# Order of the border loads, the V conversion and the kv products in an attention and MLP kernel

## The chip, the cores and the metric

The kernel runs on one core of one Trainium2 chip. The metric is device time in microseconds (us) of that core, as the median of a few runs. Engines are named as in the profile: PE (TensorE products), PEld (its weight loads), DVE (VectorE), ACT (ScalarE), POOL (GpSimd), SP (SyncE, which issues every transfer of this kernel).

## What is computed

```python
# attention without softmax, 8 batches, 8 heads, 576 rows, 64 columns
kv  = einsum('bhsd,bhse->bhde', k, v)
x   = einsum('bhsd,bhde->bhse', q, kv);  x = x / rms(x) * g_norm
# first block: low-rank mixing over the sequence, then channels 512 -> 2048 -> 512
u   = x + (x.T @ U @ V).T               # U is 576 x 32, V is 32 x 576
x   = u + maximum(u @ w_ch1, 0) @ w_ch2
# second block: gated MLP with a 576 x 576 product over the sequence
h   = gelu(x @ w_in);  uu, v = halves of h
out = x + (uu * (w_sg @ layernorm(v) + b_sg)) @ w_out
```

All is float32. U, V and the weights arrive as 64-bit floats, and the kernel turns them into float32 itself (`convert`). The large products are split into a high and a low part of each operand and done as three products (`three`: high by high, high by low, low by high).

## The kernel before

**Stages.** (1) Per batch b: kv products (`att_kv`), five chunks c of x (`att_x`), root and norm (`att_root`, `att_norm`), the low-rank mixing (`att_t` by U, `att_u` by V), and the first 6 of 16 slices of `w_ch1` (`ch1`, two units "U" a slice, one for each half of the sequence). Batch b+1's attention runs between the units of batch b, by the list `PERIOD`, and for b = 0 by the shorter list `FIRST`, since batch 1's x products are already done ahead of it. (2) The other ten slices as a seven-product scheme on blocks of 1024 tokens (`Unit`). Its results go to DRAM (`yd`). (3) `w_ch2`: nine blocks of 512 tokens with eight steps each (`ch2`, two slices f a step); the weights were converted in stage 2, kept in DRAM (`wd`) and are brought back by `load_w2`. (4) The gated MLP.

**What sets the order.** PE runs in the order in which the program stands. On the other engines and in SP's queue a planner orders at build time: among the instructions that its own timing holds ready it takes the one that stands first in the program. Each engine then runs its list strictly in that order. `behind` (`keep_in_program_order`) pins an instruction behind the instruction that stands just before it in the program on the same engine; `convert` and the stores of weight slices are pinned so. `converted` first writes out the conversion of a slice and only then, by `flush`, the store of the slice before it: the store's ACT copy and its subtraction (on POOL for odd slices f, on DVE for even ones) stand behind the next slice's conversion.

**The front, lines 470 to 525.** kv, U and V, and q of batch 0 are loaded; U is converted and stored; then both halves of V, each converted and stored (lines 485 to 488), then kv products of batch 0, `att_x(0, c)`, `att_root(0)`, kv products of batch 1, norms. The loop over `cs` does chunks 0 and 1, 2 and 3, then 4: `att_t(0, c)`, `att_x(1, c)` and, twice, `split_w` of slices 0 and 1. Then `att_u(0, d)` for four d (line 336 multiplies by V, line 344 makes the low part `ul`), `att_root(1)`, `split_w(2)`, the norms of batch 1's first chunks, `split_w(3)`. Slices 4 and 5 are split after the first and third unit of batch 0, and the last store comes after the fifth. The tile `sq` of `att_x` (line 275) has one buffer. PSUM has four buffers "ar", which the kv, x and u products share. In `FIRST`, "K2" is the kv product of batch 2's pair 2; each of K0 and K1 also issues the load of the pair after next (line 553).

**The border of stages 2 and 3, lines 693 to 807.** The last three units are interleaved, and their results leave through SP's queue. w2 slices 8 to 11 are loaded after the pair of units before them, 12 to 15 at product b7 of the last three, 0 to 7 at the border, since their tiles lie on memory of stage 2. `load_y(j, i)` brings two slices of y for a step and splits them into `yx` (ACT line 752, DVE line 753). The first block begins with i = 4, whose y and i = 5's are already on the chip (tile `y0`), so step 2 (i = 6) is the first that needs a y transfer in stage 3. `load_z1(1)` uses `y0`'s buffer.

```python
    load_y(*steps[0])
    load_z1(0)
    load_y(*steps[1])
    for f in range(8):
        load_w2(f)
    for at_, (j, i) in enumerate(steps):
        if 2 <= at_ + 1 < len(steps):
            load_y(*steps[at_ + 1])
```

Of the kernel before, what the change touches and what calls it, by code (L numbers as in the profile page):

```python
# [12 lines left out]
F32 = mybir.dt.float32  # L13
# [9 lines left out]
B, H, S, D = 8, 8, 576, 64  # L23
DM, DFF, RANK = 512, 2048, 32
# [35 lines left out]
def tile_kernel(ctx: ExitStack, tc: tile.TileContext, kvm, kvr, qt, gcol, uv, w12,  # L60
# [21 lines left out]
    def in_turn(*chains):  # L82

        end = object()
        while chains:
            chains = [steps for steps in chains if next(steps, end) is not end]
# [9 lines left out]
    def convert(raw, tmp):  # L96

        low, high = raw[:, :, 0], raw[:, :, 1]
        t = tmp.bitcast(I32)
        behind(nc.scalar.activation(tmp, high.bitcast(F32), AF.Abs))
        behind(nc.scalar.activation(low, low.bitcast(U32), AF.Copy, scale=2.0 ** -29))
        yield
        yield behind(nc.vector.tensor_scalar(tmp, tmp, 2.0 ** -15, 122879.9921875, ALU.max, ALU.min))
        yield behind(nc.vector.tensor_scalar(t, t, 3, 0x3FFFFFF8, ALU.logical_shift_left, ALU.bitwise_and))
        yield behind(nc.vector.scalar_tensor_tensor(t, high, -0x40000000, t, ALU.bitwise_and, ALU.bitwise_or))  # L108
        yield behind(nc.gpsimd.tensor_add(t, t, low))  # L109
# [9 lines left out]
    def flush():  # L119
        while queue:  # L120
            queue.pop(0)()
# [28 lines left out]
    def slot(i, shape, dt, name):  # L150

        return px["wa" if i < 14 else "xa"].tile([P] + shape, dt, tag=f"s{i}", name=f"{name}{i}")
# [49 lines left out]
    def split_w(f):  # L202
        w = slot(f, [2, DM], F32R, "w")
        wh[f], wl[f] = w[:, 0], w[:, 1]
        sub = nc.gpsimd if f % 2 else nc.vector
        converted(w_raw.pop((f, 0)), next_tmp(), split_to(w[:, 0], w[:, 1], sub))
# [39 lines left out]
    def att_kv(b, ps):  # L246
        if ps[0] == 0:
            at_s["kv", b] = pm.tile([P, NP, D], F32, tag="ar", bufs=4, name="kvps")
        acc = at_s["kv", b]
        for p in ps:  # L250
            m, r = kv_t.pop((b, p))
            for c in range(NC):
                src = m[:, c] if c < 4 else r
                for j in range(2):
                    mm(acc[j * D:(j + 1) * D, p, :], src[:, j * D:(j + 1) * D],
                       src[:, P + j * D:P + (j + 1) * D], start=(c == 0), stop=(c == NC - 1))
# [7 lines left out]
    def att_x(b, c):  # L264

        n = rows(c)
        if c == 0:
            at_s["ss", b] = small(b, "ss", 0)
            nc.gpsimd.memset(at_s["ss", b][64:, 4], 1.0)
        ps = pm.tile([P, H, D], F32, tag="ar", bufs=4, name="xps")  # L270
        for p in range(NP):
            mm(ps[:n, 2 * p:2 * p + 2, :], q_t[b, p][:, c * P:c * P + n], kvbd[:, p, :],  # L272
               start=True, stop=True)
        xn = xn_of(b, c)
        sq = ap.tile([P, H, D], F32, tag="sq", name="sq")
        nc.scalar.activation(sq[:n], ps[:n], AF.Square)
        nc.scalar.activation(xn[:n], ps[:n], AF.Copy)
        nc.vector.tensor_reduce(at_s["ss", b][:n, c], sq[:n], AX.X, ALU.add)
        at_s["x", b, c] = xn

    def att_root(b):
        ss = at_s.pop(("ss", b))
        y, t = (small(b, n, i) for i, n in ((1, "ny"), (2, "nt")))
        a, y2, t2 = (i.rearrange("p w h -> p (w h)") for i in (ss, y, t))
        nc.vector.tensor_scalar(a, a, 1.0 / D, EPS, ALU.mult, ALU.add)
        in_turn(rsqrt(y2, t2, a))
        at_s["y", b] = y

    def att_norm(b, cs):

        y = at_s["y", b]
        for c in cs:
            n = rows(c)
            xn = at_s["x", b, c]
            nc.vector.tensor_tensor(xn[:n], xn[:n], y[:n, c].unsqueeze(2).to_broadcast([n, H, D]),
                                    ALU.mult)
            xf = xn.rearrange("p h d -> p (h d)")
            xh = ap.tile([P, DM], F32R, tag="xh", bufs=2, name="xh")
            xl = xh[n:] if c == 4 else ap.tile([P, DM], F32R, tag="xl", bufs=2, name="xl")
            nc.scalar.activation(xh[:n], xf[:n], AF.Copy)  # L300
            nc.vector.tensor_sub(xl[:n], xf[:n], xh[:n].bitcast(F32))
            at_s["x", b, c] = xf, xh, xl
# [72 lines left out]
    def store_v(c, x):  # L375
        nc.scalar.activation(v4[:, c], x, AF.Copy)
        nc.gpsimd.tensor_sub(v4[64:96, c], x[64:96], v4[64:96, c].bitcast(F32))
# [104 lines left out]
    tmp_u = next_tmp()[:, :nu]  # L482
    in_turn(convert(uvr[0][:, :nu], tmp_u))
    store_u(tmp_u)
    tmp_v = [slot(i, [2, DM], F32, "tmpv")[:, 0, :HS] for i in (6, 7)]
    for h, (r, t) in enumerate(zip((uvr[0][:, nu:], uvr[1]), tmp_v)):
        in_turn(convert(r, t))
        store_v(slice(h * HS, (h + 1) * HS), t)
    att_kv(0, list(range(NP)))
    put_kv(0)  # L490
    for p in range(NP):
# [6 lines left out]
    for f in range(1, NA):  # L498
        load_w(f, 0)
    att_root(0)  # L500
    att_kv(1, list(range(NP)))
    put_kv(1)
    att_norm(0, (0, 1))
    for cs in ((0, 1), (2, 3), (4,)):
        if cs[0]:
            att_norm(0, cs)
        for c in cs:
            att_t(0, c)
        for c in cs:
            att_x(1, c)  # L510
        if cs[0] < 4:
            split_w(cs[0] // 2)
    for p in range(2):
        load_kv(2, p)
    for d in range(ND):
        att_u(0, d)
    att_root(1)
    for p in range(NP):
        load_q(2, p)
    split_w(2)  # L520
    att_norm(1, (0, 1))
    split_w(3)

    PERIOD = "X0 X1 X2 X3 U X4 U U K0 U K1 U T0 T1 U U T2 T3 U U T4 U K2 U K3 U D0 D1 D2 D3".split()
    FIRST = "U U U K0 U K1 U T0 T1 U U T2 T3 U U T4 U K2 U K3 U D0 D1 D2 D3".split()
    for b in range(B):
        n, n2 = (i if i < B else None for i in (b + 1, b + 2))
        i = 0
# [161 lines left out]
    while units:  # L690
        n = 3 if len(units) == 3 else 2
        two, units = units[:n], units[n:]
        a, b = two[0], two[-1]
        if n == 3:
            for s in "a5 a1 b5 b1 a3 a6 b3 b6 c5 c1 a7 b7 a2 c3 c6 b2 a4 c7 b4 c2 c4".split():
                two["abc".index(s[0])].product(int(s[1]))
                if s == "b7":
                    for f in range(12, 16):
                        load_w2(f)
        else:  # L700
            for x, p in ((a, 5), (a, 1), (b, 5), (b, 1), (a, 3), (a, 6), (b, 3), (b, 6), (a, 7), (b, 7),
                         (a, 2), (b, 2), (a, 4), (b, 4)):
                x.product(p)
        if b.j == len(BLOCKS) - 1 and b.i in (0, 1):
            y = up.tile([P, ND, S], F32, tag="u32", bufs=2, name="y0")
            y_at.append(y.rearrange("p d s -> p (d s)")[:, :2 * 2 * BT].rearrange("p (a f t) -> p a f t", a=2, f=2))
            for k in range(2):
                nc.sync.dma_start(y_at[0][:, k], yd[0][:, 8 + 2 * k:10 + 2 * k])
        if b.j == len(BLOCKS) - 1 and b.i == 1:
            for f in range(8, 12):  # L710
                load_w2(f)
    flush()
    pha.close()
# [25 lines left out]
    def load_z1(b):  # L739
        zt[b] = up.tile([P, ND, S], F32, tag="u32", bufs=2, name="z32")  # L740
        nc.sync.dma_start(zt[b], ud[b])
# [31 lines left out]
    steps = [(j, (i + 4) % 8) for j in range(NB) for i in range(8)]  # L773
    load_y(*steps[0])
    px["wb"] = wb = ph1.enter_context(tc.tile_pool(name="wb", bufs=1, side="left", reuse_waits="tile"))
    load_z1(0)
    load_y(*steps[1])
    for f in range(8):
        load_w2(f)
    for at_, (j, i) in enumerate(steps):  # L780
        if 2 <= at_ + 1 < len(steps):
            load_y(*steps[at_ + 1])
        step = at_ % 8
        if step == 0 and j + 1 < B:
            load_z1(j + 1)
        for k in range(2):
            ch2(j, 2 * i + k, step == 0 and k == 0, step == 7 and k == 1)
        if j == 0 and step == 5:
            raws = prepare_sg()
        if j == 1 and step < 5:  # L790
            split_sg(step, raws[step])
        if j == NB - 2 and step in (0, 1, 2, 3, 4, 5):
            if step == 0:
                load_wio(0)
            load_wio(step + 1)
            split_wio(step)
        if j == NB - 1:
            if 1 <= step < 7:
                if step < 6:
                    load_wio(step + 6)  # L800
                split_wio(step + 5)
            elif step == 7:
                flush()
            if step >= 3 and step < 7:
                split_z(0, step - 3, zt[order[0]][:, step - 3], nc.vector)
        if step == 7:
            z_out(j)
# [277 lines left out]
```

## Time and profile before

| | |
|---|---|
| median of 3 runs | 1395.4 us (1394.03 to 1396.19) |
| the profiled execution | 1394.67 us |
| its span, first to last instruction | 1392.7 us |
| PE busy | 1346.4 us, 97% of the span |
| DVE, ACT, POOL busy | 771.3, 536.5, 284.2 us |

Times within the kernel are microseconds from the start of the span. The profile holds one execution. A busy PE is one with a product in flight, whatever its clock: the granted clock (1.00 is 2.4 GHz, 0.50 is 1.2 GHz) has a column of its own.

### The profile page before, as it was taken

How to read it: one execution, taken by the hardware profiler on the slowest of the kernel's cores; microseconds unless marked ns; L12 is line 12 of the kernel's file. 1: busy time of each engine (PE TensorE's matmuls, PEld its weight loads, DVE VectorE, ACT ScalarE, POOL GpSimd, SP SyncE). 2: the span in 40 equal slices, each digit the busy share in tenths (PEclk: the TensorE clock that was granted, in tenths of full speed). 3: DMA queues.
4: the chain of work that ended last, by engine and by line, in shares of the span. 5: the costliest groups of instructions: out<-in, count | busy, mean ns of one | idle time of the engine just before them, and what ended most of it. 6: DMA issues, size and time to landing. Idle time of an engine off the chain costs nothing.

```text
span 1392.7 us, 20749 instructions
## 1 busy us (share of the span) xinstructions
PE 1346.4 (97%) x8050; PEld 1177.5 (85%) x8050; DVE 771.3 (55%) x1405; ACT 536.5 (39%) x888; POOL 284.2 (20%) x268
## 2 busy tenths in 40 slices
PE   5799999999999999899999999999999999999998
PEld 4689999997777788688888888888999999999998
DVE  3757777755766732222322223456676775775874
ACT  3656656654554532212112122454333333423321
POOL 1211111100111100200000000336253453543332
PEclk9899999999999999999999999999999999999999
DMA  9556665355766777635434554631020120110001
GB/s 325 189 165 215 220 215 179 132 174 194 252 228 223 243 268 276 238 96 170 146 118 159 163 169 145 210 122 44 1 68 19 51 69 18 52 44 26 35 17 52
DMA packets 86930, 199.44 MB, mean 143 GB/s; under 512 B 12208, under 2 KB 33456, under 8 KB 85040
## 3 DMA queue, kind: packets, MB, share of 16 engines
q1 hardware_dynamic: 86832, 198.12, 42.9%
q8 instruction: 63, 1.03, 0.3%
q14 instruction: 35, 0.29, 0.1%
HBM read 126.00 MB, written 72.09 MB: 142 GB/s over the span
## 4 chain that ended last, share of the span: by engine, by line
PE 83%; DVE 5%; DMA 3%; ACT 2%; issue 1%; POOL 1%; SPq 0%; DVEq 0%; ACTq 0%; POOLq 0%
PE acc L348 9%; PE acc L347 9%; PE acc L349 9%; PE uso L936 8%; PE uso L957 6%; PE uso L848 5%; PE c L347 3%; PE c L348 3%; PE c L349 3%; PE y L347 3%; PE y L348 3%; PE y L349 3%; PE v L347 2%; PE v L348 2%; PE v L349 2%; PE xps L272 2%
## 5 line engine op out<-in xcount | busy, mean ns | idle before, releaser
L347 PE MATMUL acc<-yx,w 128*128 128x512 f32 x576 | 225.3, 391 | 5.9 <-ACT yx L752 5.9
L348 PE MATMUL acc<-yx,w 128*128 128x512 f32 x576 | 225.7, 392 | 1.5 <-DVE yx L753 1.5
L753 DVE SCALAR_TENSOR_TENSOR yx<-yr,yx 128x1024 fp32r<-128x1024 f32 x70 | 86.1, 1230 | 254.2 <-ACT yx L752 249.8
L349 PE MATMUL acc<-yx,w 128*128 128x512 f32 x576 | 225.3, 391 | 0.0
L752 ACT ACTIVATE yx<-yr 128x1024 fp32r<-128x1024 f32 x70 | 74.3, 1061 | 286.9 <-PE acc L349 267.0
L347 PEld LDWEIGHTS acc<-yx,w 128*128 128x128 f32 x576 | 108.8, 189 | 29.3 <-ACT yx L752 6.6
L348 PEld LDWEIGHTS acc<-yx,w 128*128 128x128 f32 x576 | 108.8, 189 | 24.7 <-DVE yx L753 2.1
L349 PEld LDWEIGHTS acc<-yx,w 128*128 128x128 f32 x576 | 108.9, 189 | 22.7
L349 PE MATMUL c<-uh,w 128*128 128x288 f32 x384 | 114.0, 297 | 6.6 <-POOL w L126 6.6
L347 PE MATMUL c<-uh,w 128*128 128x288 f32 x384 | 117.2, 305 | 0.0
L348 PE MATMUL c<-ul,w 128*128 128x288 f32 x384 | 114.1, 297 | 1.8 <-DVE ul L344 1.8
L848 PE MATMUL uso<-zh,wio 128*128 128x288 f32 x512 | 94.1, 298 | 0.8 <-DVE g2u L856 0.7
L957 PE MATMUL uso<-gh,wio 128*128 128x288 f32 x512 | 93.1, 296 | 0.0
L109 POOL TENSOR_TENSOR tmp<-tmp,wior 128x512 int32<-128x512 int32 x12 | 15.7, 1307 | 332.2 <-DVE tmp L108 287.2
L957 PEld LDWEIGHTS uso<-gh,wio 128*128 128x128 f32 x512 | 77.9, 188 | 2.3 <-issue 0.2
L347 PE MATMUL y<-T,c 128*128 128x512 f32 (+1 forms) x200 | 75.3, 377 | 4.0 <-DVE y L595 3.7
L848 PEld LDWEIGHTS uso<-zh,wio 128*128 128x128 f32 x512 | 76.3, 188 | 3.4 <-PE uso L936 1.4
L349 PEld LDWEIGHTS c<-uh,w 128*128 128x128 f32 x384 | 72.6, 189 | 7.1 <-POOL w L126 7.1
L348 PEld LDWEIGHTS c<-ul,w 128*128 128x128 f32 x384 | 72.6, 189 | 3.9 <-DVE ul L344 3.0
L347 PEld LDWEIGHTS c<-uh,w 128*128 128x128 f32 x384 | 72.5, 189 | 3.2 <-issue 1.0
L349 PE MATMUL y<-T,c 128*128 128x512 f32 (+1 forms) x200 | 74.5, 372 | 0.0
L348 PE MATMUL y<-T,c 128*128 128x512 f32 (+1 forms) x200 | 74.4, 372 | 0.0
(206 smaller groups left out, 2912.4 us busy)
## 6 DMA issues: line engine op xcount, KB each, us to landing
yr<-yd SPq DMA_DIRECT2D x70, 512.0 KB, 3.6
yd<-y SPq DMA_DIRECT2D x92, 256.0 KB, 3.5
kvm<-kvm_dram SPq DMA_DIRECT2D x28, 512.0 KB, 4.6
raw<-w_dram SPq DMA_DIRECT2D x26, 512.0 KB, 4.2
q<-qt_dram SPq DMA_DIRECT2D x32, 288.0 KB, 4.6
ud<-ut SPq DMA_DIRECT2D x32, 288.0 KB, 2.2
z<-ud SPq DMA_DIRECT2D x8, 1152.0 KB, 6.9
out_dram<-ot SPq DMA_DIRECT2D x31, 288.0 KB, 2.1
```

The costliest lines, as they stand in the source:

```text
L109: yield behind(nc.gpsimd.tensor_add(t, t, low))
L272: mm(ps[:n, 2 * p:2 * p + 2, :], q_t[b, p][:, c * P:c * P + n], kvbd[:, p, :], start=True, stop=True)
L347: mm(ps, ah, bh, start=start, stop=False, **kw)
L348: mm(ps, ah, bl, start=False, stop=False, **kw)
L349: mm(ps, al, bh, start=False, stop=stop, **kw)
L752: nc.scalar.activation(yh, y, AF.Relu)
L753: nc.vector.scalar_tensor_tensor(yl, y, 0.0, yh.bitcast(F32), ALU.max, ALU.subtract)
L848: mm(ps[:, e, :HS], a[:, s], c[:, halves[e]], start=(d == 0 and i == 0), stop=(d == ND - 1 and i == 2))
L936: mm(ps[:, e, :HS], a[:, s], w[:, halves[e]], start=(c == 0 and i == 0), stop=(c == NC - 1 and i == 1))
L957: mm(ops[d][:, e, :HS], a[:, s], c[:, f, halves[e]], start=(f == 0 and i == 0), stop=(f == ND - 1 and i == 2))
```

## The change

```diff
@@ att_x
-        sq = ap.tile([P, H, D], F32, tag="sq", name="sq")
+        if b or c % 2 == 0:
+            sq = ap.tile([P, H, D], F32, tag="sq", name="sq")
+        else:
+            sq = spare[4][:, 2700:2700 + DM].rearrange("p (h d) -> p h d", h=H)
@@ the front
     store_u(tmp_u)
-    tmp_v = [slot(i, [2, DM], F32, "tmpv")[:, 0, :HS] for i in (6, 7)]
-    for h, (r, t) in enumerate(zip((uvr[0][:, nu:], uvr[1]), tmp_v)):
-        in_turn(convert(r, t))
-        store_v(slice(h * HS, (h + 1) * HS), t)
     att_kv(0, list(range(NP)))
...
     att_root(0)
+    tmp_v = [slot(i, [2, DM], F32, "tmpv")[:, 0, :HS] for i in (6, 7)]
+    uv_in = [convert(r, t) for r, t in zip((uvr[0][:, nu:], uvr[1]), tmp_v)]
     att_kv(1, list(range(NP)))
...
         if cs[0]:
             att_norm(0, cs)
+        if cs[0] == 2:
+            in_turn(*uv_in)
...
             split_w(cs[0] // 2)
+        if cs[0] == 4:
+            for h, t in enumerate(tmp_v):
+                store_v(slice(h * HS, (h + 1) * HS), t)
+            flush()
...
         att_u(0, d)
+    split_w(2)
+    split_w(3)
     att_root(1)
...
-    split_w(2)
     att_norm(1, (0, 1))
-    split_w(3)
...
-    FIRST = "U U U K0 U K1 U T0 T1 U U T2 T3 U U T4 U K2 U K3 U D0 D1 D2 D3".split()
+    FIRST = "U U K0 U K1 U U U T0 T1 U K2 U K3 T2 T3 U U T4 U U D0 D1 D2 D3".split()
@@ stage 2, after product b7 of the last three units
-                    for f in range(12, 16):
+                    for f in range(11, 14):
@@ stage 2, after the pair of units before them
-            for f in range(8, 12):
+            for f in range(8, 11):
@@ the border
     load_y(*steps[0])
-    load_z1(0)
     load_y(*steps[1])
-    for f in range(8):
-        load_w2(f)
+    later_loads = [lambda f=f: load_w2(f) for f in (14, 15)] + [lambda: load_z1(0)] + [lambda f=f: load_w2(f) for f in range(8)]
+    later_loads.pop(0)()
+    later_loads.pop(0)()
     for at_, (j, i) in enumerate(steps):
         if 2 <= at_ + 1 < len(steps):
             load_y(*steps[at_ + 1])
+        for _ in range(3):
+            if later_loads:
+                later_loads.pop(0)()
```

V is converted behind the norms of chunks 2 and 3 and stored behind chunk 4; the store of slice 1 follows there; slices 2 and 3 are split ahead of `att_root(1)`; the squares of batch 0's odd chunks get a second place; the kv products of batch 2 stand further apart. At the border the loads that the first steps don't need stand three to a step between the y loads.

## Rows read from the trace of the kernel before

**Rows 1.** The page, its first part: busy time, share, instructions.

```profile
PE 1346.4 (97%) x8050; PEld 1177.5 (85%) x8050; DVE 771.3 (55%) x1405; ACT 536.5 (39%) x888; POOL 284.2 (20%) x268
```

**Rows 2.** PE's waits: line, waited for, us in total, times, longest.

```profile
PE c L349 <- POOL w L126: 6.6, 2, 6.2
```

**Rows 3.** ACT in order of time: start, us, what, [idle before <- releaser].

```profile
19.10 0.44 ACT L376 ACTIVATE v<-tmpv 128x288 fp32r<-128x288 f32 x1 [1.80 <-POOL tmpv L109]
20.16 0.58 ACT L276 ACTIVATE sq<-xps 128x512 f32<-128x512 f32 x1
```

**Rows 4.** DVE in order of time.

```profile
27.66 0.68 DVE L278 TENSOR_REDUCE spare<-sq 64x8 f32<-64x512 f32 x1 [0.72 <-ACT sq L276]
40.76 0.43 DVE L106 TENSOR_SCALAR tmp<-tmp 128x512 f32<-128x512 f32 x1
41.69 0.69 DVE L108 SCALAR_TENSOR_TENSOR tmp<-spare,tmp 128x512 int32<-128x512 int32 x1
51.95 0.76 DVE L344 TENSOR_TENSOR ul<-ut,uh 128x576 fp32r<-128x576 f32 x1
```

**Rows 5.** PE in order of time, up to the first product by V.

```profile
14.53 7.86 PE L272 MATMUL xps<-kvbd,q 128*128 128x128 f32 x40 [1.22 <-DMA q<-qt_dram]
33.11 0.79 PE L310 MATMUL tp<-xh,u 128*128 128x512 f32 x1 [5.58 <-ACT xh L300]
43.85 0.36 PE L336 MATMUL ups<-v,t 128*128 128x256 f32 x1 [1.21 <-DVE t L316]
```

**Rows 6.** Instructions on V's temporary by stretch: DVE, ACT, POOL busy (count), clock.

```profile
16.00:24.00 8.00, 2.50 (x6) 1.68 (x4) 3.18 (x4) 1.00 1.04 321
```

**Rows 7.** All engines by stretch: PE, PEld, DVE, ACT, POOL busy, granted clock.

```profile
42.40:52.70 10.30, 7.23 (x38) 4.75 (x37) 9.52 (x19) 8.85 (x18) 2.91 (x2) 1.00 0.56 182
57.56:64.39 6.83, 3.01 (x16) 2.73 (x18) 3.74 (x8) 1.97 (x4) 3.77 (x2) 0.50 0.57 220
```

**Rows 8.** PE in order of time, units of batch 0.

```profile
54.87 0.29 PE L348 MATMUL c<-ul,w 128*128 128x288 f32 x1
61.38 0.61 PE L349 MATMUL c<-uh,w 128*128 128x288 f32 x1 [6.22 <-POOL w L126]
64.08 0.81 PE L255 MATMUL kvps<-kvm 128*64 128x64 f32 x16
79.48 0.50 PE L310 MATMUL tp<-xh,u 128*128 128x512 f32 x1 [1.01 <-DVE xh L301]
```

**Rows 9.** POOL in order of time, slices 2 and 1.

```profile
57.40 2.71 POOL L109 TENSOR_TENSOR tmp<-tmp,spare 128x512 int32<-128x512 int32 x1 [2.72 <-DMA raw<-w_dram]
60.07 1.25 POOL L126 TENSOR_TENSOR w<-tmp,w 128x512 fp32r<-128x512 f32 x1
```

**Rows 10.** Line 109 on POOL up to 95 us: durations in ns, least, median, most.

```profile
L109 POOL TENSOR_TENSOR tmp<-tmp,spare x6: 1287/1632/2709, 42.6 to 75.2; 128x512 int32<-128x512 int32 x6
```

**Rows 11.** One unit of ch1 on PE: stretch, length, PE and PEld busy.

```profile
82.38:84.16 1.78, 1.78 (x12) 1.62 (x12) 0.00 (x0) 0.00 (x0) 1.00 0.43 151
```

**Rows 12.** Transfers issued up to 95 us: count, KB each, median us to landing.

```profile
kvm<-kvm_dram SPq DMA_DIRECT2D x10, 512.0 KB, 5.3
```

**Rows 13.** SP's queue at the border in order of time.

```profile
546.70 3.35 SPq L685 DMA_DIRECT2D w<-wd  x7
550.15 0.38 SPq L741 DMA_DIRECT2D z<-ud  x1
551.10 4.19 SPq L748 DMA_DIRECT2D yr<-yd  x3
```

**Rows 14.** ACT at the border.

```profile
564.22 1.06 ACT L752 ACTIVATE yx<-yr 128x1024 fp32r<-128x1024 f32 x1 [16.34 <-DMA yr<-yd]
```

**Rows 15.** PE at the border, steps 2 to 4 of stage 3.

```profile
565.32 0.50 PE L347 MATMUL acc<-yx,w 128*128 128x512 f32 x1 [4.52 <-ACT yx L752]
570.59 0.39 PE L347 MATMUL acc<-yx,w 128*128 128x512 f32 x1
579.00 0.39 PE L348 MATMUL acc<-yx,w 128*128 128x512 f32 x1
```

## The prediction

> **What bounds the kernel now.** The first view is the page's busy time: PE works 97% of the span, with 46 us idle in all, and no other engine is over 55% [rows 1]. So only what PE waits for, or the clock at which it runs, can move the end. The second view is PE's waits. They don't spread over the kernel: the large ones lie in the first 80 us and at one place near 560 us, and the largest of the front is for POOL's low part of an odd weight slice [rows 2]. From 80 to 545 us and from 580 us on PE is busy nearly all the time, so I take it that a microsecond saved ahead of a packed stretch arrives whole at the end. The third view is the engines in order of time around each wait, the fourth SP's queue at the border.
>
> **Front, part 1: V out of the way of batch 0's squares.** In the trace the x products of batch 0 start at 14.53 and end at 22.39 [rows 5], but ACT takes the first chunk's square only at 20.16, because the store of V's first half stands ahead of it and waits for POOL until 19.10, and then the second half's conversion stands there too [rows 3]. The squares and their sums end at 27.66 + 0.68 = 28.34 [rows 4]. Root and norm follow, and PE, idle for 5.58, takes up the first product by U at 33.11 [rows 5]: 4.77 after the last sum. With V gone from there, ACT can take each chunk as PE finishes it. The last products then end at about 22.4 as now, the square takes 0.58 [rows 3], the sum 0.68: 23.7. Adding the same 4.77 gives 28.5 for the first product by U, a gain of **4.7 us**. The kv products of batch 1 fit into the time between. The second place for odd squares is part of this: with one place each square waits for the sum before it (0.72 of DVE's idle time in front of the last sum is the other side of it [rows 4]). A few tenths either way are possible, through the copies of kv into place.
>
> **Front, part 2: V's new place.** V's conversion costs DVE 2.50, ACT 1.68 and, with both subtractions, POOL 3.18 [rows 6], two ACT copies more for the store. It is pinned behind the norms of chunk 3 only, and the pieces come just when ACT and DVE wait for batch 1's x products. What doesn't fit there meets a DVE that is busy 9.52 of 10.30 us up to the last `ul` at 51.95 + 0.76 = 52.71 [rows 7, 4]. Bounds: nothing, if all fits into the idle time; 2.5, if all of DVE's work is added. The other question is when V is there: its first product is at 43.85 in the old timetable [rows 5], while the store isn't pinned and may be put behind batch 1's last square, some 3 to 4 us later. PE would wait there, but the evacuations behind it are paced by DVE anyway. I take a loss of **1.0** (0 to 4), nearer the lower end because both engines have gaps just ahead.
>
> **Front, part 3: the slices.** PE has slice 1's high part at 54.87 and then idles 6.22 for its low part [rows 8]. POOL does that subtraction at 60.07, behind the addition of slice 2's conversion, 57.40 and 2.71 long [rows 9], since a store stands behind the next conversion, and that conversion's DVE steps were pinned behind the root of batch 1. The change stores slice 1 behind chunk 4, before slice 2 is touched. Its subtraction is then over before `att_u` ends, and the 6.22 fall away. The idle time also brought the clock to 0.50 from 57.56 to 64.39 [rows 7]: the ten products of the unit from 61.38 to 64.08 took 2.70 [rows 8], against 10/12 of 1.6 to 1.78, some 1.35 to 1.5, at full clock [rows 11]. That is 1.3 more. A second wait of 0.4 for an odd slice is in the total of the same row [rows 2], and 1.01 before chunk 4's product by U [rows 8], behind slice 5's store. In sum 6.2 + 1.3 + 0.4 + 1.0 = **8.9**.
>
> What is late next: slice 2 is wanted four units and two kv products after the first unit, about 7 us after the last `ul`. Its chain from there is DVE 1.6 (40.76 to 42.38 for such a slice [rows 4]), POOL 1.3 to 2.7 [rows 10], ACT 0.6, DVE 0.7: 4.2 to 5.6. That just fits. Slice 3's subtraction stands behind slice 4's addition, and slice 4's conversion behind batch 1's first norms. I make that 10 to 13 us against a need at 11.5. The root of batch 1 now competes with two conversions (2 x 1.6 on DVE), and its norms are wanted 10 us after the last `ul`. I charge **1.0** (0 to 3) for a wait at one of these. The kv products: K0 and K1 come one unit earlier and their data is long there; K2 comes five units and two products by U after K0, some 9 us, and its load, issued behind K0, takes 5.3 [rows 12]. Nothing is charged; without that cover, up to 3.
>
> **Border.** SP issues seven w2 loads from 546.70, z at 550.15 and the three y loads from 551.10 [rows 13]. The y of step 2 is there at 564.22, 13 us after its issue, since 4.7 MB stand ahead of it [rows 14], and ACT starts at once. PE has idled 4.52 by 565.32, and in the next 5.27 us (to 570.59) it does twelve products, for which it takes 2.72 at its later pace (37 products in 8.41 us, 0.227 each) [rows 15]: part of that is the wait for DVE's half of y, part a clock that has fallen again. The whole loss is 4.52 + 2.55 = 7.1. With the change two w2 slices and z stand ahead of that y instead of eight and z, that is 1.0 + 1.2 MB instead of 5.2; slices 14 and 15 add 1.0 at most, if they aren't issued before. z still waits for `y0`'s buffer until 550.15. At the rate now seen (5.2 MB in 13 us, 0.4 MB a us) y lands at 550.6 + (1.2 + 0.5 + at most 1.0)/0.4 plus some 2 us of latency, so at 557 to 559. It is wanted 2.3 us ahead of 560.8, at 558.5. The next y has three slices ahead of it, 1.5 MB, 4 us, and each step lasts 5.4. Slices 0 to 7 are wanted from step 4 on. So I take the whole **7.1** as gained (0 to 7.1). The wait at the very start of stage 3, for the split of `y0`, stays.
>
> **Sum.** 4.7 - 1.0 + 8.9 - 1.0 + 7.1 = 18.7. The profiled execution was 1394.67, its span 1392.7, so I expect 1376.0 and a span of 1374.0; from the median of 1395.4, **1376.7**.
>
> **Rivals.** (a) *V is late.* A POOL instruction may wait for DVE: the same addition took 1.29 to 2.71 [rows 10], the longest while DVE worked beside it. The Trainium skill ("SBUF — State Buffer", "Who interferes with whom") says of this that a DVE instruction with two SBUF inputs and a GpSimd one that reads SBUF block each other for a whole instruction; the trace's spread agrees, and it speaks against putting V's additions into DVE's densest stretch. If V's four POOL steps (3.18) double, and the stores stand last in ACT's list, PE waits 4 more in front of the first product by V and the clock may fall for some 2 more: 12.7 gained, 1382.7. For it: ACT and DVE are busy 8.85 and 9.52 of 10.30 there [rows 7]. Against: POOL itself is nearly idle. (b) *The border loads don't do what they say.* The planner, not the program, orders SP's queue: if it puts y behind the w2 loads as before, or if y misses 558.5 because slices 14 and 15 and z come first, from nothing to all of the 7.1 stays: 1379 to 1384, taken as 1383.8 when all of it does. For it: y's margin is about a microsecond. (c) *Slower.* V's chain could end on the other side if its pieces, in strict lists on three engines, were put behind work that itself needs `ul`; PE would then stand in front of the first product by V. To be slower than before, that wait must eat all of 4.7 + 7.9 + 7.1, some 20 us, so V's second half would have to be stored after about 64 in the old timetable instead of 48; a wait of 24 would give 1399. Nothing in the trace shows V's own work to be above 7.4 us end to end [rows 6], so little speaks for it.
>
> **How the numbers follow.** Forecast 0.70 with its own range of 1372 to 1381; (a) 0.10; (b) 0.12; (c) 0.04; something between 0 and 10 us of gain for reasons not seen, 0.04. The range takes in (a), (b) and the terms at their good ends (5.2 + 0 + 8.9 + 0 + 7.1, with a front that keeps its clock, 22 to 24): 1371 to 1386. A measurement of this kernel tells 0.2%, 2.8 us, from no change. Faster 0.91, same 0.04, slower 0.05.
>
> **What would show it.** Right: PE's first product by U near 28.5; no wait of PE for the POOL line of odd slices over 1 us; the last `ul` near 49; the u products of batch 1 some 11 to 12 earlier; the y of step 2 landed before PE ends step 1, and no wait of PE between steps 1 and 2. Wrong: a wait of PE for V in front of line 336 of over 4 us, waits on slices 3 or 4, the clock at 0.50 in the units of batch 0, or a y of step 2 that lands later than 12 us after PE's last stage 2 product. The forecast as a whole falls if the shift isn't carried through the packed stretches, so that the stages from 92 to 545 take longer than now.

## The result and the profile after

The changed kernel takes 1380.16 us (median of 4 runs, 1378.95 to 1381.5), beside 1395.8 for the kernel before on the same chip (1394.03 to 1396.48). The ratio is 0.989, 95% interval 0.9873 to 0.9907. The profiled execution took 1380.45 with a span of 1378.4, 14.3 less than before. Predicted were 1376.7, a range of 1371 to 1386, and a span of 1374.0. So the sign and the range held, and 3 to 4 us of the 18.7 did not come.

In the changed kernel the lines up to `att_x` stand as before, the helpers from line 276 on three lines lower: the product by U is line 313, by V 339, the units 350 to 352, the split of y 759 and 760.

PE in order of time, after (start, us, what, [idle before <- releaser]): first product by U, first by V, first unit, the two small waits for slices 2 and 3, and the first transposes of batch 1's u. They stand against [rows 5, 8].

```profile
27.32 0.50 PE L313 MATMUL tp<-xh,u 128*128 128x512 f32 x1 [2.00 <-ACT xh L303]
44.80 0.58 PE L339 MATMUL ups<-v,t 128*128 128x256 f32 x1 [7.09 <-DVE nt L92]
52.25 0.44 PE L350 MATMUL c<-uh,w 128*128 128x288 f32 x1
63.35 0.40 PE L352 MATMUL c<-uh,w 128*128 128x288 f32 x1 [0.21 <-DVE w L126]
68.37 0.40 PE L352 MATMUL c<-uh,w 128*128 128x288 f32 x1 [0.64 <-POOL w L126]
81.05 0.27 PE L337 MATMUL ups<-ident,xn 128*128 128x128 f32 x1
```

DVE's last sum of squares and last `ul`, after [rows 4], and the border: ACT's and SP's lines to set against [rows 13, 14].

```profile
22.65 0.68 DVE L281 TENSOR_REDUCE spare<-sq 64x8 f32<-64x512 f32 x1 [0.26 <-ACT sq L279]
...
54.62 0.76 DVE L347 TENSOR_TENSOR ul<-ut,uh 128x576 fp32r<-128x576 f32 x1
...
542.30 0.43 SPq L755 DMA_DIRECT2D yr<-yd  x1
...
549.77 1.06 ACT L759 ACTIVATE yx<-yr 128x1024 fp32r<-128x1024 f32 x1 [7.28 <-DMA yr<-yd]
```

The landmarks put the gain in its places (us from the start of the span; "last" is the last product of stage 2, 545.29 before):

| | before | after | shift |
|---|---|---|---|
| first product by U | 33.11 | 27.32 | -5.8 |
| first product by V | 43.85 | 44.80 | +1.0 |
| first unit | 49.61 | 52.25 | +2.6 |
| first transposes of batch 1's u | 86.74 | 81.05 | -5.7 |
| last product of stage 2 | 545.29 | 539.90 | -5.4 |
| end of the span | 1392.7 | 1378.4 | -14.3 |

So the front gave 5.4 of the 11.6 that were forecast for it, the stretch from the first unit to batch 1's u products gave 8.3, the packed part from 81 to 540 kept it, and the border and what lies behind it gave 8.9. Something between 27 and 52 us took back 8.4. It stands in front of V: PE waits 7.09 there. The releaser that the row names, a small root step of DVE, is the last by the profile and not the cause. POOL's list shows what V's products waited for:

```profile
37.81 1.29 POOL L109 TENSOR_TENSOR tmp<-tmp,spare 128x512 int32<-128x512 int32 x1 [22.25 <-DVE tmp L108]
39.05 1.58 POOL L109 TENSOR_TENSOR tmpv<-tmpv,uv 128x288 int32<-128x288 int32 x2
42.33 1.51 POOL L109 TENSOR_TENSOR tmp<-tmp,spare 128x512 int32<-128x512 int32 x1 [1.70 <-ACT v L379]
43.91 1.58 POOL L380 TENSOR_TENSOR v<-tmpv,v 32x288 fp32r<-32x288 f32 x2
45.57 1.26 POOL L126 TENSOR_TENSOR w<-tmp,w 128x512 fp32r<-128x512 f32 x1
```

DVE and ACT, after, around V's conversion and store:

```profile
33.90 0.82 DVE L108 SCALAR_TENSOR_TENSOR tmpv<-uv,tmpv 128x288 int32<-128x288 int32 x2
...
36.98 0.69 DVE L108 SCALAR_TENSOR_TENSOR tmp<-spare,tmp 128x512 int32<-128x512 int32 x1
...
41.87 0.76 ACT L379 ACTIVATE v<-tmpv 128x288 fp32r<-128x288 f32 x2
```

DVE is done with both halves of V at 34.72, and POOL has been idle for 22 us. But POOL's list has slice 0's addition first, which waits for DVE until 37.67. V's additions end at 40.63, ACT copies V into place at 41.87 (behind slice 0's store and the square and copy of a chunk of batch 1), slice 1's addition stands in POOL's list ahead of V's low part, and that comes at 43.91. Each step is short and runs on an engine that is nearly idle; the order of the lists makes the chain 11 us long. Meanwhile the clock falls, and stays down for the u products and most of the first unit (stretch, PE, PEld, DVE, ACT, POOL busy, granted clock, DMA share, GB/s):

```profile
39.92:53.57 13.65, 8.77 (x32) 6.91 (x33) 12.57 (x25) 7.58 (x16) 5.16 (x6) 0.50 0.35 113
52.25:81.05 28.80, 27.10 (x235) 24.59 (x235) 17.39 (x30) 14.63 (x30) 10.39 (x6) 0.98 0.72 233
```

Before, the same 28.80 had been 37.13 long:

```profile
49.61:86.74 37.13, 28.36 (x235) 25.26 (x235) 21.47 (x43) 16.66 (x33) 11.59 (x8) 0.91 0.56 181
```

### The profile page after: what moved, and what is told of

The parts are those of the page before. It is cut to its first block, busy times and chain, and to the rows that moved or that the text cites. A ratio compares the mean times of both kernels' runs of the same rounds, so it can differ in the third digit from the quotient of the medians.

```text
span 1378.4 us, 20738 instructions
## 1 busy us (share of the span) xinstructions
PE 1343.9 (97%) x8050; PEld 1176.8 (85%) x8050; DVE 772.5 (56%) x1405; ACT 535.3 (39%) x888; POOL 286.3 (21%) x268
## 4 chain that ended last, share of the span: by engine, by line
PE 83%; DVE 5%; DMA 3%; ACT 2%; issue 1%; POOL 1%; SPq 0%; DVEq 0%; ACTq 0%; POOLq 0%
PE acc L351 10%; PE acc L352 9%; PE acc L350 9%; PE uso L946 8%; PE uso L967 6%; PE uso L858 5%; PE c L350 4%; PE c L352 3%; PE c L351 3%; PE y L350 3%; PE y L351 3%; PE y L352 3%; PE v L350 2%; PE v L351 2%; PE v L352 2%; PE xps L272 2%
```

## The experiments

Each changes a few lines of the changed kernel. "Front" is the first transposes of batch 1's u, "last" the last product of stage 2. Each ratio is against runs of the kernel before that were taken beside that kernel (their medians are 1394.76 to 1395.82), and its 95% interval is 2 to 2.5 us to either side. Landmarks are those of one execution each, and these scatter: the kernels with V moved and two squares have next to the same work up to the first product by U and reach it at 26.27 to 27.50, and e1, with the front of the kernel before, ends that front 1.0 later. So a microsecond in this table carries no verdict by itself.

| kernel | median | ratio, 95% interval | by U | by V | unit | front | last | span |
|---|---|---|---|---|---|---|---|---|
| before | 1395.8 | | 33.11 | 43.85 | 49.61 | 86.74 | 545.29 | 1392.7 |
| after | 1380.16 | 0.9873 to 0.9907 | 27.32 | 44.80 | 52.25 | 81.05 | 539.90 | 1378.4 |
| e1 border alone | 1388.42 | 0.9929 to 0.9963 | 32.72 | 44.42 | 50.19 | 87.75 | 547.77 | 1388.4 |
| e2 front alone | 1389.48 | 0.9947 to 0.9977 | 27.12 | 44.82 | 52.27 | 81.08 | 540.36 | 1388.3 |
| e3 slice 0 behind V | 1379.0 | 0.9871 to 0.99 | 26.91 | 39.74 | 47.45 | 78.92 | 538.90 | 1377.5 |
| e4 V stored early too | 1382.87 | 0.9898 to 0.9927 | 26.76 | 40.61 | 47.59 | 82.32 | 541.29 | 1380.8 |
| e5 and slice 3 stored | 1377.65 | 0.9859 to 0.9889 | 27.50 | 41.35 | 49.04 | 78.40 | 537.07 | 1374.9 |
| e6 slice 0 behind chunk 4 | 1379.45 | 0.9871 to 0.9901 | 26.27 | 38.34 | 44.85 | 77.69 | 536.66 | 1377.3 |
| e7 old `FIRST` | 1386.2 | 0.9919 to 0.9949 | 27.18 | 44.65 | 52.10 | 85.47 | 545.17 | 1384.9 |
| e8 slice 1 stored late | 1385.68 | 0.9903 to 0.9939 | 27.11 | 44.75 | 52.20 | 85.02 | 545.11 | 1385.7 |
| e9 slices behind the root | 1380.63 | 0.9879 to 0.9909 | 26.44 | 44.04 | 51.48 | 80.31 | 539.95 | 1379.3 |
| e10 one square | 1382.21 | 0.9884 to 0.9917 | 28.63 | 45.80 | 53.24 | 82.24 | 540.73 | 1380.9 |
| e11 V in its old place | 1380.98 | 0.9879 to 0.9912 | 30.77 | 42.49 | 48.77 | 81.38 | 539.97 | 1379.1 |
| e12 e5, first y in halves | 1375.72 | 0.9845 to 0.9875 | 26.83 | 40.70 | 47.66 | 77.01 | 536.04 | 1373.0 |

### The two halves of the change: e1, e2

e1 is the kernel before with the changed border, e2 the changed front with the old border.

> The kernel before with the border edits alone (w2 slices, z and y loads in threes). Theory: the border gives the whole difference of stage 3, 8.9 us (7.1 for the y wait with its fall of the clock, 1.8 for the low clock right behind the start of stage 3 that the kernel after doesn't show), the front nothing: 1387. Rival: the 1.8 hang on how the front's shift lies against the clock's state and don't come by themselves: 1388.7. Second rival: border and front help each other only together, then it is under 5 us.

> The kernel after with the border edits undone. Theory: the front gives 5.5 us by itself (last product of stage 2 at 540.2 instead of 545.6), the border's waits are all back: 1390.3. Rival: part of the gain of the front is lost at the border, because y waits for the same loads: above 1392.

The border alone gives 0.9946 and the front alone 0.9962, some 7.5 and 5.3 us; together the change gives 15.3 by its ratio. The 2.5 more lie within the three intervals. In e1 PE doesn't wait for the y of step 2. In e2 it does:

```profile
560.31 0.79 PE L350 MATMUL acc<-yx,w 128*128 128x512 f32 x1 [6.01 <-ACT yx L759]
```

From the last product of stage 2 to the end of the span it is 847.4 us before, 848.0 in e2, 840.6 in e1 and 838.5 in the changed kernel. So the border is worth 6.8 by itself. The other 2 us come and go, most of them with the clock behind the start of stage 3, where every one of these kernels but the last has the same two stalls of PE, 1.42 and 0.76, for the split of the first y. Two windows of 3.30 us behind them (before, after):

```profile
549.10:552.40 3.30, 3.30 (x9) 2.57 (x8) 0.23 (x1) 0.00 (x0) 0.00 (x0) 0.50 1.01 410
```

```profile
542.90:546.20 3.30, 3.30 (x15) 2.74 (x16) 1.04 (x1) 0.00 (x0) 0.00 (x0) 1.00 1.00 335
```

Nine products instead of fifteen: six products at 0.227, 1.4 us. The clock fell at this place in the profiles of before, e1, e4, e6, e7, e8 and e10 and not in those of after, e2, e3, e5, e9, e11 and e12. In all of them but e12 the stalls are equal, so they alone don't decide it. What does was not settled. Of the expectations, e1's rival (1388.7) and e2's theory (1390.3) came closest.

### V's wait: e3, e4, e5, e6

e3 takes slice 0's split out of chunks 0 and 1 and puts it behind V's conversion, so that POOL's list has V first:

```diff
         if cs[0] == 2:
             in_turn(*uv_in)
+            split_w(0)
...
-        if cs[0] < 4:
-            split_w(cs[0] // 2)
+        if cs[0] == 2:
+            split_w(1)
```

> The kernel after, slice 0 split behind V's conversion instead of ahead of it, so that POOL's list has V's two additions ahead of slice 0's. Theory (V is late because its additions stand on POOL behind an addition that waits for DVE until 37.7, though DVE has V ready at 34.7): V's additions start near 35, PE's wait in front of the first product by V (7.1 us in the kernel after) falls to 2 to 4, the low clock behind it shrinks: 1373 to 1376. Rival (DVE, busy nearly all the time there, sets the pace): PE waits less but the last low part of u comes at the same time, 1380 within 1.

POOL, e3: V's additions, slice 0's, V's low parts.

```profile
34.09 1.84 POOL L109 TENSOR_TENSOR tmpv<-tmpv,uv 128x288 int32<-128x288 int32 x2 [18.84 <-DMA kvm<-kvm_dram]
37.07 1.74 POOL L109 TENSOR_TENSOR tmp<-tmp,spare 128x512 int32<-128x512 int32 x1 [1.14 <-ACT xn L280]
38.89 1.55 POOL L380 TENSOR_TENSOR v<-tmpv,v 32x288 fp32r<-32x288 f32 x2
```

The first product by V comes at 39.74 with no wait, 5.1 earlier, and the first unit 4.8 earlier. So the place of slice 0 ahead of V was the cause of the 7.09. The edit moves slice 0 in the lists of DVE and ACT too; V's additions, ready for POOL as early as before, start 5.0 earlier, and that is POOL's list. But a part of the wait moves to the product by U of chunk 4, whose xh now stands behind slice 0's conversion on DVE:

```profile
37.71 0.50 PE L313 MATMUL tp<-xh,u 128*128 128x512 f32 x1 [2.04 <-DVE xh L304]
```

The clock is at 0.50 from 39.35 to 56.42, and only 2.1 of the 4.8 are left at batch 1's u products, 1.0 at the last product of stage 2. The medians, 1379.0 and 1380.16, can't be told apart, so the theory's 1373 to 1376 missed; the rival's 1380 fits the time, but not its reason, since the first unit did come earlier.

e4 stores V at the same place too, ahead of slice 0:

```diff
             in_turn(*uv_in)
+            for h, t in enumerate(tmp_v):
+                store_v(slice(h * HS, (h + 1) * HS), t)
+            split_w(0)
```

> As the run before, and V's stores stand right behind V's conversion instead of behind chunk 4. Theory: V is stored before 40, PE's wait for it is gone up to the wait for the low part of t (about 1.2, as in the kernel before), the clock stays high in the products by V and the first unit: 1370 to 1374. Rival (DVE sets the pace): 1380 within 1; if V's two copies delay the squares of batch 1 on ACT, up to 1 slower than the run before.

Both expectations missed. PE no longer waits for V, but it waits 3.29 for DVE's low part of t in front of that product. The first unit is as early as in e3, 47.59, and then slice 3 is late:

```profile
67.19 0.61 PE L352 MATMUL c<-uh,w 128*128 128x288 f32 x1 [3.73 <-POOL w L126]
```

POOL, e4: slice 4's addition and then slice 3's low part.

```profile
63.80 2.11 POOL L109 TENSOR_TENSOR tmp<-tmp,spare 128x512 int32<-128x512 int32 x1 [5.85 <-ACT xh L303]
65.87 1.26 POOL L126 TENSOR_TENSOR w<-tmp,w 128x512 fp32r<-128x512 f32 x1
```

Slice 3's low part stands behind slice 4's addition, which waits for DVE until 63.57 (the releaser that the row names is another): the pattern that the change had removed for slice 1, and the one that the prediction's "what is late next" described. PE wants slice 3's low part at 63.46 here and has it at 67.13. In the changed kernel it wants it at 67.73 and has it at 68.32, in e3 at 65.52 and 66.17: there the units start as early, but the clock stays at 0.50 for 4.0 us longer, so they run slower. The clock here is at 0.50 from 66.08 to 72.91. e5 adds the one line that the pattern asks for:

```diff
     split_w(2)
     split_w(3)
+    flush()
     att_root(1)
```

> As the run with V stored early, and slice 3's store stands right behind its conversion instead of behind slice 4's. Theory (with V out of the way, the next thing late is slice 3's subtraction, which stood on POOL behind an addition that DVE fed only after batch 1's norms): the wait of 3.7 us and the fall of the clock behind it go, the u products of batch 1 begin at 77 to 78 instead of 82.3, total 1375 to 1378. Rival (units are bound by DVE's work as a whole, not by this order): another slice or a norm becomes late by as much, 1381 to 1384.

No wait for a slice is left, batch 1's u products begin 3.9 earlier than in e4, at 78.40, and the median is 5.2 lower, with one line between the two and intervals that don't meet. The theory held. (e4's profile has the fall of the clock at the border and e5's has not, so some 1.4 of that may not be the line's.) A wait of 2.93 for the low part of t is left in front of the first product by V.

e6 moves slice 0 further, behind chunk 4's norms.

> As the run before, and slices 0 and 1 are both split behind chunk 4's product by U, so that neither stands ahead of the copy and the low part of t. Theory: the first product by V comes near 38 (40.6 with V stored early, 44.8 in the kernel after), the first unit 1 to 2 us sooner if slice 0 isn't late itself: 1373 to 1377. Rival: slices 0 and 1 become late, PE waits in the first units 2 to 5: 1378 to 1383.

The first unit comes at 44.85, 7.4 earlier than after and 4.2 earlier than in e5, but batch 1's u products only 0.7 earlier than e5's. The time between is DVE's:

```profile
45.00:55.00 10.00, 6.63 (x23) 5.40 (x24) 9.86 (x19) 5.74 (x11) 4.65 (x3) 0.51 0.66 213
```

DVE is busy 9.86 of 10, PE waits 2.06 and 0.62 for `ul`, at half the clock. The median, 1379.45, missed the theory and can't be told from e5's; it lies in the rival's range, but no slice is late. A first unit ahead of what DVE can feed brought next to nothing here.

### V's new place and the second square: e11, e10

> The changed kernel with V converted and stored in its old place ahead of the kv products of batch 0, the rest of the change kept. Theory (the move of V takes as much from the front as it gives, since V then comes last in the lists of POOL and ACT): the first product by U at 33 as in the kernel before, but no wait of PE for V, the first unit at 49 to 50 instead of 52.25, the u products of batch 1 at 79 to 80.5 instead of 81.05, the median 1377 to 1379. Rival (the earlier squares are worth the 4.7 of the sum, and V's wait is only what would have been DVE's work anyway): the first unit at 53 or later and the median 1383 or more.

e11 puts V back ahead of the kv products of batch 0. Theory and rival both missed, but for the wait for V, which is gone as the theory had it. The first product by U comes at 30.77 (before 33.11, so the second square place alone gives 2.3 with V in the way), and the first unit is at 48.77, 3.5 ahead of the changed kernel. Yet batch 1's u products are no earlier, 81.38. In e11 the clock is at 0.50 from 50.44 to 57.27, inside the units, where PE has work, and slice 3 is late:

```profile
50.56:57.39 6.83, 6.26 (x26) 5.16 (x27) 6.71 (x19) 3.46 (x8) 1.36 (x1) 0.51 0.87 289
```

```profile
68.70 0.40 PE L352 MATMUL c<-uh,w 128*128 128x288 f32 x1 [1.67 <-POOL w L126]
```

In the changed kernel most of the low stretch lies on the wait for V and on u products that DVE paces. So the move of V as it was made is worth nothing that can be measured, 0.8 us between medians whose ranges overlap. No run has e5's store of slice 3 with V in its old place, so what the move is worth in that order was not shown.

e11 also tells something of the units. It has the changed kernel's stores and order of units, and yet takes 32.61 from the first unit to batch 1's u products, not 28.80:

```profile
48.77:81.38 32.61, 29.39 (x233) 26.40 (x234) 22.72 (x43) 16.74 (x34) 9.43 (x8) 0.90 0.69 223
```

So the 8.3 that this stretch gained in the changed kernel hang in part on V's lateness: units that start later find the slices further on (slice 3 is waited for 0.64, against 1.67 in e11) and most of the low clock behind them.

e10 takes the second place for the squares away.

> The changed kernel with one place for the squares of batch 0, as before the change; V's later place and all else stay. With V in its old place and two squares the first product by U came at 30.77, against 33.11 in the kernel before and 27.32 in the changed one. Theory (each half of that part moves the front of batch 0 by some 2 us, but what PE gains ahead of V's first product it loses in front of it, because V's place in POOL's list sets that): the first product by U at 28.5 to 30, the first product by V at 44.80 within 0.7, the wait in front of it 1 to 2.5 us shorter than 7.09, the first unit within 1 us of 52.25, the median 1379 to 1381.5. Rival (V's additions on POOL follow the norms of batch 0, so a later front moves V too): the first product by V at 46.5 or later and the median 1382 or more.

The first product by U comes at 28.63, as the theory had it, 11.71 behind the first square instead of 10.17: 1.5 later. V's additions on POOL come 0.8 later, the first product by V 1.0, and batch 1's u products 1.2. PE's wait is split:

```profile
40.47 0.49 PE L310 MATMUL tp<-xh,u 128*128 128x512 f32 x1 [2.89 <-DVE xh L301]
...
45.80 0.58 PE L336 MATMUL ups<-v,t 128*128 128x256 f32 x1 [2.96 <-DVE ss L285]
```

V's place moves with the front, so most of the loss stays, against the theory; it looks like the rival's mechanism at about half of its size, though shifts of 0.8 to 1.2 are no larger than the scatter above. 1382.21 is 2.05 over the changed kernel, and the intervals overlap; the profile has the clock's fall at the border too (at 0.50 from 543.35 to 546.77), worth some 1.4.

### The order of the units and the stores: e7, e8, e9

e7 is the changed kernel with the old `FIRST`, e8 without the `flush()` behind chunk 4, e9 with slices 2 and 3 split at their old places.

> The kernel after with the kv products of batch 2 back at their places before (the old list FIRST). Theory: the units' order is worth little, since the kv loads are there in time either way and the slices' places in the list hardly move: within 1.5 of 1380. Rival: the first products by U of batch 1 come one unit earlier and wait for norms or for slice 3: 1382 to 1384.

> The kernel after without the store of slice 1 behind chunk 4 (it is then written behind slice 2's conversion, as before). Theory: the wait of PE for slice 1's low part is back with 3 to 5 us and drags slices 2 and 3, 1384 to 1388. Rival: V's lateness hides it, 1380 within 1.

> The changed kernel with slice 2's split back behind the root of batch 1 and slice 3's back behind its first norms; the stores of slice 1 behind chunk 4 and all else stay. Theory (PE stands in front of the first product by V until 44.80, and in that time DVE does root and slices in either order; what counts is only that slice 3's subtraction is over before 68): the first product by V within 1 us of 44.80, slice 3's wait 1 to 3 us instead of 0.64, the median 1380 to 1383. Rival (the place ahead of the root carries a good part of the slices' gain, since slice 2's low part stands behind slice 3's conversion): a wait of 3 us or more on slice 2 or 3 and a fall of the clock behind it, the median 1384 or more.

From the first unit to batch 1's u products the changed kernel takes 28.80, e7 33.37, e8 32.82, e9 28.83, the kernel before 37.13. So of the 8.33 that this stretch gained, taking away the order of the units costs 4.6, taking away the store of slice 1 behind chunk 4 costs 4.0, and the places of slices 2 and 3 nothing. The first two add up to about the gain. All three were taken away with V late; what they are worth with V early was not measured. What PE waits for, e7 (two rows) and e8:

```profile
68.65 0.40 PE L352 MATMUL c<-uh,w 128*128 128x288 f32 x1 [1.08 <-POOL w L126]
...
73.29 0.50 PE L315 MATMUL tp<-xl,u 128*128 128x512 f32 x1 [1.83 <-DVE xl L304]
```

```profile
61.41 0.61 PE L352 MATMUL c<-uh,w 128*128 128x288 f32 x1 [2.56 <-POOL w L126]
```

In the old order the products by U of batch 1's chunks 2 and 3 stand one unit and two kv products earlier; PE waits 1.83 for chunk 3's xl, and the clock is at 0.50 from 73.76 to 77.18. In e8 the low part of slice 1 again stands behind slice 2's addition, and the clock is at 0.50 from 60.54 to 67.36. Either one costs its wait and the fall behind it; the theory missed for e7, whose rival named both waits (at 1382 to 1384), and held for e8 (1384 to 1388), with a wait of 2.56 where it said 3 to 5. Both profiles also have the border's fall, and the medians are 6.0 and 5.5 over the changed kernel. The executions of e8 spread over 6 us (1381.48 to 1387.57), its interval just touches the changed kernel's, and the profiled one is its slowest; so 4.0 is what the late store costs in an execution whose clock falls behind it. What it costs in the others no trace shows.

e9 has the waits of the changed kernel, 0.23 and 0.64, where its theory had 1 to 3 for slice 3; its median, 1380.63, is as the theory said.

### The start of stage 3: e12

e12 is e5 with the first y split in two halves, so that ACT and DVE hand PE 512 columns at a time:

```diff
+        for r in (slice(0, 1), slice(1, 2)) if (j, i) == (0, 4) else (slice(0, 2),):
-        nc.scalar.activation(yh, y, AF.Relu)
-        nc.vector.scalar_tensor_tensor(yl, y, 0.0, yh.bitcast(F32), ALU.max, ALU.subtract)
+            nc.scalar.activation(yh[:, r], y[:, r], AF.Relu)
+            nc.vector.scalar_tensor_tensor(yl[:, r], y[:, r], 0.0, yh[:, r].bitcast(F32), ALU.max, ALU.subtract)
```

> The version with V stored behind slice 0's place and slice 3 stored ahead of the root of batch 1 (1377.65), and in it the split of the first step's y in stage 3 done in two halves of 512 columns, ACT and DVE each. Theory (the two stalls of 1.42 and 0.76 at the start of stage 3 are ACT's and DVE's pass over 1024 columns, of which the first products need 512): they shrink to 0.9 and 0.2 or less, 1.0 us saved, the median 1376 to 1377.5. Rival (ACT's first pass starts only behind its evacuation of the last stage 2 block, and the stall is that and not the pass; or the clock, which falls or stays by where the stall lies, moves more than the stall itself): no gain, or up to 1.7 us of loss, 1377.5 to 1379.5.

```profile
537.31 0.50 PE L350 MATMUL acc<-yx,w 128*128 128x512 f32 x1 [0.99 <-ACT yx L762]
538.04 0.50 PE L351 MATMUL acc<-yx,w 128*128 128x512 f32 x1 [0.23 <-DVE yx L763]
```

The two stalls shrink from 1.42 and 0.76 to 0.99 and 0.23, 0.96 us, about as expected. The span is 1.9 shorter than e5's; the other 1.0 was there at the last product of stage 2 already and belongs to the front of that execution. 1375.72 is the lowest median here, 0.986 of the kernel before (0.9845 to 0.9875); the interval overlaps e5's.

## Why the prediction came out as it did

**Front, part 1 (earlier squares, 4.7): right.** The last sum ended at 23.33 against a forecast of 23.7, the first product by U came at 27.32 against 28.5. The gain was 5.8; the chain from the last sum to that product was shorter than the 4.77 that I carried over, 4.0. e10 and e11 split it: without the second place 1.3 of it is gone, with V in the way 3.5.

**Front, part 2 (V's new place, 1.0 lost): this is the step that failed.** With 4.7 gained and 1.0 lost, V's first product was due at 40.2. It came at 44.80, 4.6 later, and the u products behind it took 7.45 up to the first unit instead of 5.76, 1.7 more. Together that is 6.3 on top of the 1.0 charged. The sign of being wrong that the prediction had set, a wait of over 4 us in front of the product by V, came (7.09), and the last `ul` ended at 55.38 instead of about 49. Of V's two questions the prediction costed DVE's time and looked for V's store behind ACT's squares. It did not follow V's four POOL steps through POOL's list, where slice 0's and slice 1's additions stand ahead of two of them each. That could have been read from the diff: V's conversion stands behind slice 0's split, and its store behind slice 1's. How much of the front's shortfall (5.4 of 11.6) this step explains is less clear than where the wait came from: with V's wait gone, e3 got 2.1 of it back at batch 1's u products, and e5, with slice 3 stored as well, 2.7.

**Rival (a)** had this size: 4 more in front of V, some 2 for the clock. Its cause was another one, though. It had POOL's additions slowed by DVE, and the stores last in ACT's list. V's two additions took 1.58 (0.79 each), as V's steps did before (3.18 for four [rows 6]); in other executions they took up to 2.30 (e10), 0.7 more. The stores did wait 1.24 in ACT's list. The rest of the time went to the place of V's steps in POOL's list, as e3 shows. The Trainium skill ("SBUF — State Buffer", "Who interferes with whom"), on which that rival leaned, was not what decided here.

**Front, part 3 (slices, 8.9, less 1.0): right in sum, in part by luck, and wrong in its parts.** 8.3 measured against 7.9, but with units that started 2.6 later than before; in e11, where they start at 48.77, the same order and stores gain 4.5. The prediction gave all of it to the store of slice 1 and charged the moved kv products at nothing. e7 and e8, with V late, show 4.0 for the store and 4.6 for the order of the units: without the new order the 6.2 of PE's wait would have come back by half, as waits for slice 3 and for batch 1's xl, with another fall of the clock. That the xl would be wanted too early was named ("wanted 10 us after the last `ul`"), but charged at 1.0; "without that cover, up to 3" was the bound for the kv products, and 4.6 lies outside it. Slice 3's margin (10 to 13 against 11.5) was judged rightly: 0.64 of a wait after, 3.73 in e4, where PE wants it 4.3 us sooner. K2's load was indeed hidden.

**Border (7.1 of 7.1): right.** No wait between steps 1 and 2 is left; e1 alone gives 6.8. y landed at 549.77, issued at 542.30: 7.5 us, against the forecast's 6.4 to 8.4 from 550.6 on, and 9.9 after the last product of stage 2, within the bound of 12. SP's list came out otherwise than the program: three w2 loads stood ahead of that y, and z behind it, where the forecast had two and z. Eight w2 loads were issued ahead of the last results of stage 2, as before the change, so that regrouping in stage 2 moved nothing. The changed kernel's profile gained 1.8 more here, since the clock did not fall behind the first two stalls. This was not forecast, and it is luck, since the clock fell there in half of the kernels' profiles. With the 1.2 more of part 1 it would account for a time below the 1382.7 of rival (a).

**Rival (c)** would have needed V 20 us late. It was 4.6 late. **The packed stretches** kept the shift, as assumed: 5.7 at 81 us, 5.4 at 540.

**What stays open.** Removing V's wait (e3) and the next one (e5) moves the front to 78.40, and e12's to 77.01, against the forecast 75.1. In e3, e5 and e12 the clock is at 0.50 for 17.1, 13.7 and 10.2 us around the u products, with PE busy for 16.2, 12.8 and 9.9 of it and DVE for 14.1, 11.4 and 9.3; which of the two holds the rest was not told apart. Nor was what makes the clock fall behind the same two stalls in some executions and not in others.

## What to carry to other kernels

When work is moved onto an engine that is nearly idle, read that engine's list, not its load: a step takes its place behind what stands ahead of it in the program, and waits for what that waits for. Of an edit that removes a wait, ask for the next wanted thing on each list: here one reordering was worth as much as the store it stood beside, and one further store (e5 against e4) was worth 4 us of the front. Parts of a sum that lie one behind the other are not independent: V's lateness hid waits that come back when the units start early (e4, e11). A wait on PE is priced with the stretch of low clock that it leaves, as far as PE has work in that stretch.

## What had not been expected of the hardware

Small DVE steps are held while POOL works beside them. In the root of batch 1 a step with two inputs on 128x40 takes 0.20; while POOL did V's and slice 1's subtractions (43.91 to 46.83) the same steps took 0.67 to 1.31 (DVE, after):

```profile
43.32 0.56 DVE L288 TENSOR_SCALAR ss<-ss 128x40 f32<-128x40 f32 x1
...
44.84 0.72 DVE L93 SCALAR_TENSOR_TENSOR nt<-nt,ss 128x40 f32<-128x40 f32 x1
45.59 1.31 DVE L94 SCALAR_TENSOR_TENSOR ny<-nt,ny 128x40 f32<-128x40 f32 x1
46.93 0.20 DVE L92 TENSOR_TENSOR nt<-ny 128x40 f32<-128x40 f32 x1
```

The 1.31 covers POOL's next subtraction of 1.26 in full. The Trainium skill ("SBUF — State Buffer", "Who interferes with whom") says that a DVE instruction with two inputs in SBUF and a GpSimd one that reads SBUF exclude each other for a whole instruction, and the rows of lines 93 and 94 agree: each ends within 0.1 us of POOL's subtraction. The first row is a step with one input: it took 0.56, against 0.18 in the root of batch 0 with POOL idle, and ended at 43.88, just behind POOL's addition (42.33 to 43.84), so two inputs are not the whole account. The prediction had weighed this for POOL's steps alone; it is DVE's chain of small dependent steps that loses more by it, some 2 us here, of which it was not shown how much reaches PE.
